# Turning q by a transposing DMA instead of TensorE, with x written in a strided order

**Chip, cores, metric.** One core of a Trainium2 chip. The metric is the device time in microseconds (us) of one execution. A profile's span is some 2 us shorter than the time of the same run.

## The reference

Attention over pooled keys and values, then a feed-forward layer with GELU. Eight batches, eight heads, 576 tokens, head dimension 64; keys and values are averaged over 8 tokens, so there are 72 of each.

```python
k_p = k.reshape(B, H, Sp, 8, D).mean(axis=3)
v_p = v.reshape(B, H, Sp, 8, D).mean(axis=3)
attn = softmax(q @ k_p^T / sqrt(D))
x = (attn @ v_p).transpose(0, 2, 1, 3).reshape(4608, 512)
out = gelu_tanh(x @ w_in) @ w_out          # w_in 512 x 2048, w_out 2048 x 512
```

## The kernel before

The second part runs in nine groups of 512 columns of x (kept transposed, as `xT`). Each group has a first layer (`w_in`, then GELU on ScalarE) and a second layer (`w_out`). Batches 1 to 7 of the attention are threaded into the groups: group g prepares batch g+1 during its first layer and computes that batch's scores, softmax and `xT` columns between the matmuls of its second layer. Batch 0 is done before group 0.

For the scores, q must lie with the head dimension on the partitions. Before, TensorE turned it, 18 transposes of 128x128 for each batch, and VectorE copied the result out of PSUM into token order:

```python
def trans_q(b, i, t0, n, bank, eng):
    if b not in qTs:
        qTs[b] = bp.tile([128, 2, 4, 32, TP], BF16, name="qT")
    tp = half_bank(bank)[:, 0:n * 128].rearrange("p (t h c) -> p h c t", h=4, c=32)
    for x in range(n):
        nc.tensor.transpose(out=half_bank(bank)[:, x * 128:(x + 1) * 128],
                            in_=qs[b][:, i, (t0 + x) * 128:(t0 + x + 1) * 128],
                            identity=identb)
    o = qTs[b][:, i, :, :, t0:t0 + n]
    ...                                    # nc.vector.tensor_copy(out=o, in_=tp)

def norm(b, c, pr, bank):                  # reciprocal of the softmax sums
    ld = ep.tile([128, CH], F32, name="ld")
    if b:
        nc.scalar.activation(out=ld[0:64], in_=PS[64:128, bank, :CH], func=ACT.Ln)
        nc.scalar.activation(out=ld[64:128], in_=PS[0:64, bank + 1, :CH], func=ACT.Ln)
    ...
    nc.scalar.activation(out=rc, in_=ld, func=ACT.Exp, scale=-1.0)

def mult(b, c, pr, bank):                  # "the multiply": writes x; CH = 288
    ...
        nc.vector.tensor_tensor(out=xT[rows, pr, col:col + CH], in0=PS[rows, bank + x, :CH],
                                in1=rc[rows], op=ALU.mult)
```

The softmax here doesn't subtract the row's maximum and nothing guards it: scores larger than these inputs give would overflow.

## Time and profile before

| | before |
|---|---|
| time, median of 3 | 320.53 us (319.16 to 321.37) |
| TensorE (PE) busy | 95% of the span |
| VectorE (DVE) busy | 55% |
| mean granted TensorE clock | 1.000 |

Page of the kernel before, costliest groups; the columns are line, engine, operation, output and inputs, shapes, count, then busy us and mean ns of one, then the engine's idle time just before them and what ended most of it:

```profile
L241 DVE TENSOR_TENSOR xT<-PS,rc 64x288 bf16<-64x288 f32 (+1 forms) x120 | 54.7, 455 | 34.5 <-ACT rc L233 24.7
```

A multiply takes 455 ns. PE's own waits in this kernel (the view of waits; us in total, times, longest):

```profile
PE PS L179 <- DMA qb<-in_q_dram: 9.6, 2, 8.9
PE PS L196 <- ACT e L202: 0.9, 3, 0.5
```

Apart from the start of the program, where the first q is awaited, and 0.7 us for the next q in group 0, PE waits for next to nothing.

### The profile page before, as it was taken

The page shows a single profiled execution, that of the slowest core. Times are in us where ns is not written, and L with a number is a line of the kernel's source. Part 1 is how long each engine was busy: PE and PEld are TensorE (multiplying, and loading weights), DVE is VectorE, ACT ScalarE, POOL GpSimd, SP SyncE. Part 2 cuts the span into 40 slices and gives each one's busy share as a digit, 9 for nine tenths or more (in the row PEclk, how much of TensorE's full clock was granted, in tenths as well). Part 3 has the DMA queues.
Part 4 walks back from the last instruction along what each step waited for, and adds up shares of the span by engine and source line. Part 5 has one row for each costly group of instructions (what it writes and reads, how often), then busy time and mean ns, then how long its engine had stood idle before and what let it go on. Part 6 is the DMA issues. An engine that isn't in the chain of part 4 may idle for free.

```text
span 318.6 us, 4265 instructions
## 1 busy us (share of the span) xinstructions
PE 301.7 (95%) x1593; PEld 156.7 (49%) x1624; DVE 176.3 (55%) x326; ACT 222.2 (70%) x414; POOL 29.5 (9%) x48
## 2 busy tenths in 40 slices
PE   0699999999999999999999999999999999999995
PEld 0456455454555455445555554555455544444442
DVE  2865836578559845974677467755776560010011
ACT  1585669967897689768985898679867987405500
POOL 8511320021001010101001100000000000000000
PEclk9999999999999999999999999999999999999999
DMA  7999999987722663174418351001200110021021
GB/s 230 262 256 261 227 259 191 248 259 175 175 74 93 165 143 107 38 221 122 125 35 222 90 147 46 0 10 59 66 2 0 66 68 0 18 83 34 0 66 66
DMA packets 17112, 37.50 MB, mean 118 GB/s; under 512 B 2020, under 2 KB 6116, under 8 KB 16196
## 3 DMA queue, kind: packets, MB, share of 16 engines
q0 software_dynamic: 10160, 24.26, 33.3%
q1 hardware_dynamic: 6708, 12.32, 12.0%
q10 hardware_dynamic: 224, 0.66, 0.5%
q8 instruction: 12, 0.20, 0.3%
q14 instruction: 8, 0.07, 0.1%
HBM read 36.70 MB, written 9.44 MB: 145 GB/s over the span
## 4 chain that ended last, share of the span: by engine, by line
PE 82%; DMA 8%; ACT 5%; POOL 3%; issue 1%; DVE 0%; ACTq 0%; POOLq 0%
PE PS L266 36%; PE PS L275 35%; DMA qb<-in_q_dram 8%; PE PS L196 4%; PE PS L215 4%; PE PS L179 2%; ACT e L202 1%; ACT ld L229 1%; ACT ld L228 1%; POOL w_in_b L101 1%; ACT gT L272 1%; PE PS L162 1%; ACT rc L233 1%; POOL kT L120 0%; POOL qb L82 0%
## 5 line engine op out<-in xcount | busy, mean ns | idle before, releaser
L266 PE MATMUL PS<-xT,w_in_b 128*128 128x512 bf16 (+2 forms) x576 | 133.8, 378 | 0.9
L275 PE MATMUL PS<-w_out_b,gT 128*128 128x512 bf16 x561 | 133.9, 379 | 0.5
L272 ACT ACTIVATE gT<-PS 128x512 bf16<-128x512 f32 x144 | 81.7, 602 | 53.3 <-PE PS L266 51.9
L266 PEld LDWEIGHTS <-w_in_b 128*128 128x128 bf16 x592 | 57.2, 99 | 60.1 <-issue 1.5
L275 PEld LDWEIGHTS <-gT 128*128 128x128 bf16 x576 | 56.0, 97 | 56.8 <-issue 0.4
L241 DVE TENSOR_TENSOR xT<-PS,rc 64x288 bf16<-64x288 f32 (+1 forms) x120 | 54.7, 455 | 34.5 <-ACT rc L233 24.7
L280 DVE COPY osb<-PS 128x512 f32<-128x512 f32 x36 | 24.9, 692 | 84.0 <-PE PS L275 84.0
L202 ACT ACTIVATE e<-PS 72x576 bf16<-72x576 f32 x64 | 40.8, 643 | 8.4 <-PE PS L196 7.5
L135 DVE TENSOR_TENSOR vt<-vt 72x1024 f32<-72x1024 f32 (+1 forms) x32 | 30.5, 952 | 0.7
L233 ACT ACTIVATE rc<-ld 128x288 f32<-128x288 f32 x64 | 28.3, 443 | 2.0
L196 PE MATMUL PS<-qT,kT 128*72 128x288 bf16 x128 | 27.6, 304 | 1.2 <-ACT e L202 0.9
L186 DVE COPY qT<-PS 128x640 bf16<-128x640 bf16 (+1 forms) x30 | 22.2, 768 | 3.3 <-PE PS L179 2.9
L228 ACT ACTIVATE ld<-PS 64x288 f32<-64x288 f32 x56 | 22.8, 407 | 1.4
L229 ACT ACTIVATE ld<-PS 64x288 f32<-64x288 f32 x56 | 22.5, 402 | 1.4
L247 ACT ACT_TABLE_LOAD x17 | 21.8, 1283 | 2.0 <-issue 1.8
L215 PE MATMUL PS<-e,vp 72*128 72x288 bf16 x112 | 23.1, 285 | 0.0
L179 PE MATMUL PS<-identb,qb 128*128 128x128 bf16 x144 | 13.9, 231 | 9.6 <-DMA qb<-in_q_dram 9.6
L196 PEld LDWEIGHTS <-kT 128*72 128x72 bf16 x128 | 15.1, 118 | 15.1 <-issue 2.1
L135 DVE TENSOR_TENSOR kt<-kt 128x1280 f32<-128x1280 f32 (+1 forms) x16 | 18.5, 1158 | 5.3 <-DMA kt<-in_k_dram 4.8
L179 PEld LDWEIGHTS <-qb 128*128 128x128 bf16 x144 | 11.2, 104 | 16.5 <-DMA qb<-in_q_dram 10.1
L168 DVE COPY kT<-PS 64x504 bf16<-64x504 bf16 x15 | 10.1, 675 | 9.4 <-PE PS L162 9.3
L215 PEld LDWEIGHTS <-vp 72*128 72x128 bf16 x112 | 11.0, 98 | 3.3
(40 smaller groups left out, 77.4 us busy)
## 6 DMA issues: line engine op xcount, KB each, us to landing
kt<-in_k_dram POOLq DMA_DIRECT2D x7, 1024.0 KB, 10.6
vt<-in_v_dram POOLq DMA_DIRECT2D x6, 1152.0 KB, 9.8
out_dram<-osb SPq DMA_DIRECT2D x24, 256.0 KB, 2.1
qb<-in_q_dram POOLq DMA_DIRECT2D x7, 576.0 KB, 10.9
w_in_b<-in_moe_w_in_dram POOLq DMA_DIRECT2D x4, 512.0 KB, 20.4
w_out_b<-in_moe_w_out_dram POOLq DMA_DIRECT2D x4, 512.0 KB, 22.2
out_dram<-osb SPq DMA_DIRECT2D x8, 192.0 KB, 2.2
vt<-in_v_dram SPq DMA_DIRECT2D x2, 576.0 KB
```

The costliest lines, as they stand in the source:

```text
L135: nc.vector.tensor_tensor(out=o, in0=a, in1=b, op=ALU.add)
L179: nc.tensor.transpose(out=half_bank(bank)[:, x * 128:(x + 1) * 128], in_=qs[b][:, i, (t0 + x) * 128:(t0 + x + 1) * 128], identity=identb)
L196: nc.tensor.matmul(out=PS[:Sp, bank + e, :CH], lhsT=kTs[b % 2][:, c, h, :], rhs=qTs[b][:, h // 4, h % 4].rearrange("p c t -> p (c t)"), st ...
L202: nc.scalar.activation(out=e, in_=PS[:Sp, bank:bank + 2, :CH], func=ACT.Exp, scale=1.0 / 64.0)
L215: nc.tensor.matmul(out=PS[:, bank + x, :CH], lhsT=flat(vps[b % 2][:, pr, x]), rhs=e[:, x, :], start=True, stop=True)
L228: nc.scalar.activation(out=ld[0:64], in_=PS[64:128, bank, :CH], func=ACT.Ln)
L229: nc.scalar.activation(out=ld[64:128], in_=PS[0:64, bank + 1, :CH], func=ACT.Ln)
L233: nc.scalar.activation(out=rc, in_=ld, func=ACT.Exp, scale=-1.0)
L241: nc.vector.tensor_tensor(out=xT[rows, pr, col:col + CH], in0=PS[rows, bank + x, :CH], in1=rc[rows], op=ALU.mult)
L266: nc.tensor.matmul(out=PS[:, h_bank(g, fo), c0:c1], lhsT=w_in_b[:, ko, fo * 128:(fo + 1) * 128], rhs=xT[:, ko, r0 + c0:r0 + c1], start=(ko ...
L272: nc.scalar.activation(out=gTs[g][:, fo, :], in_=PS[:, h_bank(g, fo), :], func=ACT.Gelu_apprx_tanh)
L275: nc.tensor.matmul(out=PS[:, o_bank(g, r), :], lhsT=gTs[g][:, fo, r * 128:(r + 1) * 128], rhs=w_out_b[:, fo, :], start=(fo == 0), stop=(fo ...
```

## The change

The intent: take 126 transposes off PE, the bound, and 28 copies off VectorE, by letting a DMA on the sync queue turn q of batches 1 to 7 while the first layer runs. The DMA gives the tokens of a chunk in another order (t, p instead of p, t). The score matmul therefore reads nine runs of 32 elements and computes its 288 columns in that order, and the multiply puts the columns back into token order as it writes `xT`. Core of the diff (the placing of some VectorE steps in the schedule is cut):

```diff
+    def trans_q_dma(b):
+        qTs[b] = bp.tile([128, 2, TP, 128], BF16, name="qT")
+        nc.sync.dma_start_transpose(out=qTs[b].rearrange("p i t c -> p (i t) c"),
+                                    in_=qs[b].rearrange("p i c -> p (i c)"))
@@ qk
-                             rhs=qTs[b][:, h // 4, h % 4].rearrange("p c t -> p (c t)"),
+                             rhs=qTs[b][:, h // 4, :, h % 4 * 32:h % 4 * 32 + 32],
@@ mult
-            nc.vector.tensor_tensor(out=xT[rows, pr, col:col + CH], in0=PS[rows, bank + x, :CH],
-                                    in1=rc[rows], op=ALU.mult)
+            nc.vector.tensor_tensor(
+                out=xT[rows, pr, col:col + CH].rearrange("p (c t) -> p t c", t=TP),
+                in0=PS[rows, bank + x, :CH].rearrange("p (t c) -> p t c", t=TP),
+                in1=rc[rows].rearrange("p (t c) -> p t c", t=TP), op=ALU.mult)
@@ group loop
-            tq = [lambda a=a, i=i: trans_q(nb, *a, 4 + i, nc.vector) for i, a in enumerate(QG)]
+            trans_q_dma(nb)
```

Successive elements of the result lie TP = 9 elements, 18 bytes, apart.

More of the change, by code (lines that the diff above doesn't have):

```diff
@@ L175, in trans_q @@
         if b not in qTs:
-            qTs[b] = bp.tile([128, 2, 4, 32, TP], BF16, name="qT")
-        tp = half_bank(bank)[:, 0:n * 128].rearrange("p (t h c) -> p h c t", h=4, c=32)
+            qTs[b] = bp.tile([128, 2, TP, 128], BF16, name="qT")
+        tp = half_bank(bank)[:, 0:n * 128].rearrange("p (t c) -> p t c", c=128)
         for x in range(n):
@@ L181, in trans_q @@
                                 identity=identb)
-        o = qTs[b][:, i, :, :, t0:t0 + n]
+        o = qTs[b][:, i, t0:t0 + n]
         if eng is nc.scalar:
@@ L186, in trans_q @@
             nc.vector.tensor_copy(out=o, in_=tp)
+    def trans_q_dma(b):
+        qTs[b] = bp.tile([128, 2, TP, 128], BF16, name="qT")
+        nc.sync.dma_start_transpose(out=qTs[b].rearrange("p i t c -> p (i t) c"),
+                                    in_=qs[b].rearrange("p i c -> p (i c)"))
     QG = [(0, 0, 5), (0, 5, 4), (1, 0, 5), (1, 5, 4)]
@@ L195, in qk @@
             h = 2 * pr + e
-            nc.tensor.matmul(out=PS[:Sp, bank + e, :CH], lhsT=kTs[b % 2][:, c, h, :],
-                             rhs=qTs[b][:, h // 4, h % 4].rearrange("p c t -> p (c t)"),
+            nc.tensor.matmul(out=PS[:Sp, bank + e, :CH].rearrange("j (t p) -> j t p", p=32),
+                             lhsT=kTs[b % 2][:, c, h, :],
+                             rhs=qTs[b][:, h // 4, :, h % 4 * 32:h % 4 * 32 + 32],
                              start=True, stop=True)
@@ L335 @@
             v0, v1 = v_steps(nb, 0), v_steps(nb, 1)
-            tq = [lambda a=a, i=i: trans_q(nb, *a, 4 + i, nc.vector) for i, a in enumerate(QG)]
+            trans_q_dma(nb)
             tk = [lambda: trans_k(nb, 4)]
             if g:
-                plan = {2: kk[:1], 3: kk[1:], 4: tq[:1], 5: tq[1:2], 6: tq[2:3], 7: tq[3:],
-                        9: tk, 10: v0[:1], 11: v0[1:], 12: v1[:1], 13: v1[1:]}
+                plan = {2: kk[:1], 3: kk[1:], 7: v0[:1], 8: v0[1:], 9: tk, 11: v1[:1], 12: v1[1:]}
             else:
-                plan = {1: v0, 2: v1, 7: kk, 8: tq[:1], 9: tq[1:2], 10: tq[2:3], 11: tq[3:], 13: tk}
+                plan = {1: v0, 2: v1, 7: kk, 12: tk}
             for fo, what in plan.items():
```

## The prediction

> **What bounds the kernel now.** I read the page first for the busy shares and the chain that ended last, then the PE timeline of one steady group, then the same stretch of group 0, where the loads are still coming in, and last the landing times of transfers.
>
> ```profile
> PE 301.7 (95%) x1593; PEld 156.7 (49%) x1624; DVE 176.3 (55%) x326; ACT 222.2 (70%) x414; POOL 29.5 (9%) x48
> ...
> PE 82%; DMA 8%; ACT 5%; POOL 3%; issue 1%; DVE 0%; ACTq 0%; POOLq 0%
> ```
>
> PE is the bound and DVE is not: PE has no idle slice after the start and makes up 82% of the chain. So DVE time that is removed is worth nothing by itself, and PE time that is removed is worth its full length, as long as nothing new makes PE wait. In nanoseconds per row PE durations overlap (a 512-column matmul shows 379 ns, but eight follow each other in 1.73 us, 216 ns apart), so I take the cost of the transposes from start times. In a steady group (the timeline of PE, first columns start and length):
>
> ```profile
> 132.28 0.44 PE L179 MATMUL PS<-identb,qb 128*128 128x128 bf16 x5
> 132.56 1.03 PE L266 MATMUL PS<-xT,w_in_b 128*128 128x512 bf16 x4
> 133.42 0.39 PE L179 MATMUL PS<-identb,qb 128*128 128x128 bf16 x4
> 133.64 1.03 PE L266 MATMUL PS<-xT,w_in_b 128*128 128x512 bf16 x4
> 134.50 0.44 PE L179 MATMUL PS<-identb,qb 128*128 128x128 bf16 x5
> ```
>
> Five transposes push the next matmul by 132.56 - 132.28 = 0.28 us, four by 133.64 - 133.42 = 0.22 us. The reader is to see that 18 transposes cost 2 x 0.28 + 2 x 0.22 = 1.0 us, not 18 x 231 ns = 4.2 us. Group 0 has one more thing, a wait for the load of q of batch 1:
>
> ```profile
> 36.10 0.45 PE L179 MATMUL PS<-identb,qb 128*128 128x128 bf16 x5 [0.73 <-DMA qb<-in_q_dram]
> ...
> 44.73 0.41 PE L196 MATMUL PS<-qT,kT 128*72 128x288 bf16 x2
> ```
>
> That load lands at 36.1 us and its first score matmul runs at 44.73 us. How long a transfer from the sync queue takes depends on when it is sent. These are the stores of 256 KB (last column: us from issue to landing), first in the stretch 36 to 60 us, then from 125 us to the end:
>
> ```profile
> out_dram<-osb SPq DMA_DIRECT2D x2, 256.0 KB, 12.2
> ...
> out_dram<-osb SPq DMA_DIRECT2D x16, 256.0 KB, 2.0
> ```
>
> The same store takes six times as long while the software queue is full of loads. The view by stretches shows the DMA engines oversubscribed (share 1.20) from 36 to 43.4 us, 1.01 from 43.4 to 61.6, 0.89 from 61.6 to 77, and about 0.45 in the later groups.
>
> **What the Trainium skill says.** "VectorE: DVE Perf Modes", section "The three transpose paths", lists 390 ns for TensorE and 1309 ns for the DMA crossbar per 128x128 block; the trace has 219 to 231 ns for one TensorE transpose and 56 ns between starts, so here the matmul way is far cheaper than listed. No transposing DMA is in the trace. "DMA: Bandwidth & Descriptors", section "Latency and other measured facts", gives 261 GB/s for one transposing kernel; its section "DMA Transpose (X-bar)" puts one crossbar tile at 16 partitions by 128 elements. Its section "Queues, rings and completion order" says that each DMA engine takes turns between queues packet by packet; the 12.2 against 2.0 us above agree with a sync transfer that gets a turn only between packets of a long software backlog. "SBUF — State Buffer", section on the DMA port swizzle, warns of a penalty for accesses that step to a new 16-byte line each time. The trace speaks mildly against it for VectorE: the qT copies read PSUM 256 bytes apart and write runs of five, and still take 820 ns for 640 elements and 716 ns for 512, about 0.8 ns per further element.
>
> **The change, part by part.**
>
> Removed from PE: 18 transposes in each of seven groups, 7 x 1.0 = 7.0 us, all on the path. Also the 0.7 us wait of group 0 at 36.1 us. Together 7.7 us, which is 2.4% of 320.5. This is the ceiling.
>
> Removed from DVE: 28 copies of 768 ns, 21.5 us, all off the path, worth nothing. The POOL wait for these transposes before the next q load turns into a wait for the DMA transpose; those loads come a whole group early, so it is worth nothing either.
>
> The score matmul reads 9 runs of 32 elements in place of 288 in a row; a run is 64 bytes, so whole lines are used. I expect no change (0.12 us between starts). The multiply writes x with a step of 18 bytes. I expect 455 ns as now, by the qT copies. If it slowed by 0.3 us, only the four multiplies right after a group's end matter: they end 2.8 us after the next first-layer matmuls begin (127.70 to 130.50), and the columns of the second half are needed in groups 1 to 3 only. That would be 3 x 1.2 = 3.6 us at most.
>
> Added: seven transposing DMAs of 576 KB. In groups 1 to 6 one is issued behind the last store of the group before, about 0.9 us after the group's start, and needed by the first score matmul, at 144.35 us for a group begun at 127.70: 16.65 us, less the 1.0 us saved, less 0.9, so a window of 14.8 us. The engines are almost idle early in that window (share 0.16 from 128 to 134 us). At 261 GB/s the estimate is 2.3 us plus about 2 us, the landing of a small transfer. Even three times this is hidden.
>
> In group 0 the window is short. q lands at 36.1; the scores would be due at 44.73 - 0.73 - 1.0 = 43.0 us, a window of 6.9 us. There are 144 crossbar tiles, nine for each of 16 engines, an estimate from the skill's tile size. The 256 KB store has eight rows of 2 KB per engine and took 12.2 us in this crowd, 1.5 us a turn. Nine turns give 13.7 us, by bytes (36 KB against 16 KB an engine) it would be 27 us, on quiet engines about 5. I choose 13: landing at 49, a PE stall of 6 us. Nothing later gives it back, as PE is the bound in every later group.
>
> Sum: 320.5 - 7.0 - 0.7 + 6 = 318.8; the stall drains the backlog somewhat, so that group 1 stays hidden; I say 318.5.
>
> **The rivals.**
>
> First: everything is hidden. For it: most score windows are 15 us, and SBUF to SBUF needs no HBM. Against it: the 12.2 us stores in the crowded stretch. It would make 320.5 - 7.7 = 312.8.
>
> Second: the transposing DMA is slow in itself. If 18 blocks of 1309 ns ran one after another they would take 23.6 us, 9 us over the window in each of six groups and 17 or more in group 0: 320.5 - 7 + 54 + 17 = 385. For it: small pieces, 32 bytes per partition and tile on the writing side, and nobody in this trace shows its rate. Against it: 32 KB in 1309 ns looks like one engine's pace, and there are 16. A milder case, 17 us, costs about 2 us a group and 10 us at the start: 320.5 - 7.7 + 12 + 10 = 335.
>
> Third: DVE's strided write or PE's broken reads are slower. At most 3.6 us for the first, as above; it would eat half the gain and leave about 316 to 322 depending on group 0.
>
> **Range and chances.** Faster by over 2% means below 314.1: at least 6.4 of the 7.7 us must remain, so group 0 may stall 1.3 us at most, that is its transpose must land within about 8 us in a stretch where a smaller store took 12. I give 0.22. Slower by over 2% means above 326.9, which needs a group 0 transpose over 21 us or a steady one over 16 us: 0.25. Between them 0.53. The range is 312.5 (everything hidden) to 334 (the milder slow case).
>
> **What would show it.** Right: PE without the q transposes but for batch 0, first matmuls of groups 2 to 6 without gaps and each such group 1.0 us shorter (33.1 to 32.1 us), the transposes landing inside 15 us there, over 10 us in group 0, with one PE wait of 3 to 9 us on qT near 43 us. The multiplies stay near 455 ns and the score matmuls near 0.12 us apart. Wrong: a wait on qT in every group (the second rival), no wait in group 0 (the first), multiplies of 600 ns or more (the third), or stores held up behind a transpose in the sync queue so long that a copy out of PSUM waits for its buffer.

## The result

| | before | after |
|---|---|---|
| time, median | 320.95 us (4 runs) | 432.51 us (4 runs) |
| PE busy | 95% | 73% |
| VectorE busy | 55% | 63% |
| the multiply | 455 ns | 1434 ns |
| mean granted TensorE clock | 1.000 | 0.925 |

The ratio is 1.3485 (95% interval 1.342 to 1.3551). The change costs 112 us; 318.5 was predicted and 334 was the top of the range.

Page of the kernel after: busy times, then the chain that ended last by engine, then the group of the multiplies:

```profile
PE 315.9 (73%) x1470; PEld 150.5 (35%) x1498; DVE 270.3 (63%) x298; ACT 222.4 (52%) x414; POOL 29.6 (7%) x48
...
PE 41%; DVE 35%; DMA 10%; issue 7%; ACT 7%; ACTq 0%; DVEq 0%
...
L247 DVE TENSOR_TENSOR xT<-PS,rc 64x288 bf16<-64x288 f32 (+1 forms) x120 | 170.0, 1434 | 42.8 <-PE PS L221 34.5
```

VectorE, absent from the chain before, now makes up 35% of it, and one line does most of that: the multiply (30% of the chain by the page), three times as long. PE's waits after:

```profile
PE PS L221 <- DVE xT L247: 42.3, 42, 1.2
PE PS L201 <- DMA qT<-qb: 26.4, 1, 26.4
PE PS L274 <- DVE xT L247: 25.8, 13, 3.1
...
PE PS L226 <- DVE xT L247: 1.4, 2, 0.8
```

There are two separate losses. The first is 42.3 + 25.8 + 1.4 = 69.5 us of waiting for multiplies: L221, the matmul with v, waits for the PSUM bank that a multiply still reads, and L274, the first layer of the next group, waits for columns of x. The second is one single wait of 26.4 us for the transposed q, in group 0. What a steady second layer looks like, busy us of each engine in one such stretch, before and after (then the granted clock, the DMA share and GB/s):

```profile
143.06:160.83 17.77, 17.66 (x96) 9.60 (x97) 9.07 (x19) 15.89 (x32) 0.86 (x1) 1.00 0.42 111
```

```profile
207.85:233.29 25.44, 18.98 (x95) 9.51 (x96) 19.18 (x15) 16.50 (x34) 0.39 (x1) 1.00 0.31 78
```

The same 96 or so matmuls take 25.44 instead of 17.77 us. The third figure with a count is VectorE: 19.18 us of work with fewer instructions, where there were 9.07. VectorE has become the bound of this stage: from its first multiply on, at 213.57 us, its timeline has no gap until 232.5 us. The first part of it:

```profile
213.57 5.80 DVE L247 TENSOR_TENSOR xT<-PS,rc 64x288 bf16<-64x288 f32 x4 [0.64 <-ACT rc L239]
219.41 0.69 DVE L288 COPY osb<-PS 128x512 f32<-128x512 f32 x1
220.13 5.80 DVE L247 TENSOR_TENSOR xT<-PS,rc 64x288 bf16<-64x288 f32 x4
```

And the transposing DMA itself, us from issue to landing, in the stretch 30 to 40 us (group 0), then the median over all seven:

```profile
qT<-qb SPq DMA_TRANSPOSE x1, 34.5
```

```profile
qT<-qb SPq DMA_TRANSPOSE x7, 5.1
```

On quiet engines it is nearly as fast as predicted (4.3 us). In group 0 it takes 34.5 us where 13 was guessed and the window was about 7. PE, which had nothing else to do, found its clock at half when it came back: in the profile's stretches the granted clock is 0.50 from 49.3 to 69 us and 0.86 from 69 to 80.

Of the 112 us, 69.5 + 26.4 are waits that the view names and 7.7 were saved as planned. Some 24 us more are left by subtraction. Most of that is the lower clock, which came with both faults: in each later group, too, it is at 0.50 for 3.4 or 6.8 us, about when PE's wait for columns of x ends (239.4 to 242.8 us, for one). Over the ten stretches at 0.50 in the change PE is busy for 35.4 us by the view by stretches. Half of that, 17.7 us, is an estimate of what the clock cost; some 6 us stay open. The kernel before had a mean clock of 1.000.

### The profile page after: what moved, and what is told of

Its sections match the earlier page's. It is cut to its first block, busy times and chain, and to the rows that moved or that the text cites. A ratio compares the mean times of both kernels' runs of the same rounds, so it can differ in the third digit from the quotient of the medians.

```text
span 430.2 us, 3997 instructions
## 1 busy us (share of the span) xinstructions
PE 315.9 (73%) x1470; PEld 150.5 (35%) x1498; DVE 270.3 (63%) x298; ACT 222.4 (52%) x414; POOL 29.6 (7%) x48
## 4 chain that ended last, share of the span: by engine, by line
PE 41%; DVE 35%; DMA 10%; issue 7%; ACT 7%; ACTq 0%; DVEq 0%
DVE xT L247 30%; PE PS L274 24%; PE PS L283 13%; DMA qT<-qb 8%; DVE osb L288 3%; ACT e L208 2%; ACT rc L239 2%; ACT ld L234 2%; DMA kt<-in_k_dram 2%; PE PS L201 1%; ACT ld L235 1%; PE PS L221 1%; DVE vt L135 1%; PE PS L162 1%; DVE kt L135 1%
## 5 line engine op out<-in xcount | busy, mean ns | idle before, releaser
L247 DVE TENSOR_TENSOR xT<-PS,rc 64x288 bf16<-64x288 f32 (+1 forms) x120 | 170.0, 1434 | 42.8 <-PE PS L221 34.5
L274 PE MATMUL PS<-xT,w_in_b 128*128 128x512 bf16 (+2 forms) x579 | 141.6, 400 | 26.6 <-DVE xT L247 25.8
L283 PE MATMUL PS<-w_out_b,gT 128*128 128x512 bf16 x561 | 136.1, 384 | 0.8 <-issue 0.2
L274 PEld LDWEIGHTS <-w_in_b 128*128 128x128 bf16 x592 | 60.6, 104 | 102.6 <-issue 31.8
L221 PE MATMUL PS<-e,vp 72*128 72x288 bf16 x112 | 29.6, 286 | 44.2 <-DVE xT L247 42.3
L201 PE MATMUL PS<-qT,kT 128*72 128x288 bf16 x128 | 27.1, 296 | 27.9 <-DMA qT<-qb 26.4
L168 DVE COPY kT<-PS 64x504 bf16<-64x504 bf16 x15 | 10.1, 675 | 17.9 <-PE PS L162 17.8
L70 POOL DMA_DIRECT2D kt<-in_k_dram x7 | 4.0, 574 | 143.6 <-DVE kp L135 141.5
L221 PEld LDWEIGHTS <-vp 72*128 72x128 bf16 x112 | 10.5, 99 | 9.1 <-issue 5.1
L179 PE MATMUL PS<-identb,qb 128*128 128x128 bf16 x18 | 2.3, 311 | 8.8 <-DMA qb<-in_q_dram 8.8
L82 POOL DMA_DIRECT2D qb<-in_q_dram x9 | 6.4, 710 | 29.7 <-DMA qT<-qb 28.5
```

The costliest lines, as they stand in the source:

```text
L201: nc.tensor.matmul(out=PS[:Sp, bank + e, :CH].rearrange("j (t p) -> j t p", p=32), lhsT=kTs[b % 2][:, c, h, :], rhs=qTs[b][:, h // 4, :, h ...
L221: nc.tensor.matmul(out=PS[:, bank + x, :CH], lhsT=flat(vps[b % 2][:, pr, x]), rhs=e[:, x, :], start=True, stop=True)
L247: nc.vector.tensor_tensor(out=xT[rows, pr, col:col + CH].rearrange("p (c t) -> p t c", t=TP), in0=PS[rows, bank + x, :CH].rearrange("p (t ...
L274: nc.tensor.matmul(out=PS[:, h_bank(g, fo), c0:c1], lhsT=w_in_b[:, ko, fo * 128:(fo + 1) * 128], rhs=xT[:, ko, r0 + c0:r0 + c1], start=(ko ...
L283: nc.tensor.matmul(out=PS[:, o_bank(g, r), :], lhsT=gTs[g][:, fo, r * 128:(r + 1) * 128], rhs=w_out_b[:, fo, :], start=(fo == 0), stop=(fo ...
```

## Experiments

The theories at this point. **W**: a scattered two-byte write is slow by itself. Rivals: **R**, the three-dimensional operands or their reads cost it; **C**, collisions with TensorE's reads or with DMA do. **Q**: the transpose of group 0 is slow because its pieces wait their turn among the loads of the software queue (those that GpSimd issues); rivals: **S**, a start-up cost, and **X**, the crossbar (what does the transposing in the DMA) suffers beside other traffic. All runs gave correct results. e1, e7, e8, e9 and e12 are one run each and are read for single operations, not for their total time.

### e1: the multiply by itself

Appended behind the last store of the kernel before, where nothing else runs, on scratch tiles:

```diff
+    for _ in range(4): nc.vector.tensor_tensor(out=bx[:, 0:CH], in0=bp0, in1=ba, op=ALU.mult)
+    # and 18 more: result in the change's order; reads in steps, write dense (both inputs, PSUM
+    # alone, SBUF alone); bf16 at steps 2, 3, 4, 8, 9, 16; f32 at steps 2, 4, 9; pairs and fours
+    # 16 bytes apart; a VectorE cast and two ScalarE casts
```

> The kernel before, with 19 small VectorE and ScalarE operations on scratch appended after its last store, four of each, on quiet engines: the multiply of 64x288 with its result written dense, in the order of the change (18 bytes from element to element), at other steps and in float32, with strided reads and a dense write, and copies. Theory W (the scattered two-byte write is slow by itself): dense 455 ns, the change's write 1430 ns with nothing else running, strided reads with a dense write near 455 ns. Rival R (the three-dimensional operands or the reads cost it): strided reads with a dense write are slow too. Rival C (collisions with TensorE reads or DMA): the change's write is near 455 ns here. Among the steps: if a new 16-byte line per element is what costs, steps of 2 and 4 elements (4 and 8 bytes) are fast or in between and 8 and more are slow; if any separate two-byte write costs, 2 is as slow as 9.

Durations in ns (min/median/max), one line for each variant. In order: dense; the change's order; both inputs in steps of 128 bytes with a dense write; only the PSUM input so; only the SBUF input so; bf16 at steps of 2, 4 and 8 elements; f32 at a step of 4 elements (16 bytes); pairs of bf16 16 bytes apart; ScalarE dense and in the change's order:

```profile
L408 DVE TENSOR_TENSOR by<-PS,ba x4: 449/449/450, 316.9 to 318.3; 64x288 bf16<-64x288 f32 x4
L409 DVE TENSOR_TENSOR by<-PS,ba x4: 1411/1412/1412, 318.8 to 323.1; 64x288 bf16<-64x288 f32 x4
L410 DVE TENSOR_TENSOR by<-PS,ba x4: 623/624/625, 324.6 to 326.6; 64x288 bf16<-64x288 f32 x4
L411 DVE TENSOR_TENSOR by<-PS,ba x4: 449/449/450, 327.2 to 328.7; 64x288 bf16<-64x288 f32 x4
L412 DVE TENSOR_TENSOR by<-PS,ba x4: 623/625/626, 329.2 to 331.1; 64x288 bf16<-64x288 f32 x4
L413 DVE TENSOR_TENSOR by<-PS,ba x4: 470/470/471, 331.8 to 333.3; 64x288 bf16<-64x288 f32 x4
L415 DVE TENSOR_TENSOR by<-PS,ba x4: 786/787/789, 336.5 to 338.9; 64x288 bf16<-64x288 f32 x4
L416 DVE TENSOR_TENSOR by<-PS,ba x4: 1422/1423/1424, 339.8 to 344.1; 64x288 bf16<-64x288 f32 x4
L420 DVE TENSOR_TENSOR by<-PS,ba x4: 652/657/658, 358.8 to 360.9; 64x288 f32<-64x288 f32 x4
L422 DVE TENSOR_TENSOR by<-PS,ba x4: 449/449/451, 364.4 to 365.8; 64x288 bf16<-64x288 f32 x4
L425 ACT CAST by<-PS x4: 392/392/392, 374.0 to 375.3; 64x288 bf16<-64x288 f32 x4
L426 ACT CAST by<-PS x4: 1408/1408/1409, 375.7 to 380.0; 64x288 bf16<-64x288 f32 x4
```

W holds: 1412 ns with every other engine idle, so C falls; the reads explain at most 175 ns, so R falls for the bulk. Three things were new. Steps through PSUM are free, steps through float32 in SBUF are not (449 against 625). ScalarE suffers as VectorE does (392 to 1408). And pairs of bf16 in separate 16-byte lines cost nothing, while singles cost everything: it is not the new line alone. That became e12. (Seven of the 19 variants are not shown here.)

### e12: half words

```diff
+    # pairs 16 bytes apart, on a word, then shifted by one element; threes 16 bytes apart;
+    # 144 and 72 single elements 18 bytes apart; 288 singles in the upper half of a word
```

> Six more multiplies on scratch behind the kernel before, all writing bf16 with f32 inputs. Theory H (a four-byte word of which only one half is written costs about 4.4 ns for each 16-byte line touched): pairs on a word, 16 bytes apart, 449 ns; the same pairs shifted by one element, so that each fills two half words, about 790; threes 16 bytes apart about 575; 144 single elements 18 bytes apart about 790 and 72 about 470; 288 single elements 16 bytes apart, in the upper half of the word, 1420. Theory L (the new line costs, not the half word): shifted pairs and threes 449.

In order: pairs on a word, shifted pairs, threes, 144 singles:

```profile
L407 DVE TENSOR_TENSOR by<-PS,ba x4: 450/450/451, 315.8 to 317.3; 64x288 bf16<-64x288 f32 x4
L408 DVE TENSOR_TENSOR by<-PS,ba x4: 787/787/789, 317.8 to 320.2; 64x288 bf16<-64x288 f32 x4
L409 DVE TENSOR_TENSOR by<-PS,ba x4: 576/577/579, 321.0 to 322.9; 64x288 bf16<-64x288 f32 x4
L410 DVE TENSOR_TENSOR by<-PS,ba x4: 776/778/779, 323.5 to 325.9; 64x144 bf16<-64x144 f32 x4
```

A pair that fills a four-byte word: 450 ns. The same pair shifted so that it fills two halves: 787. Theory H holds in every variant (72 singles gave 466, the upper half 1422). VectorE's bf16 results of the two runs fit one rule, worked out from them: time = 150 ns + the larger of 1.04 ns per element and 4.4 ns per 16-byte line in which some four-byte word is only half written. (Singles 4, 6, 8 and 16 bytes apart touch 72, 108, 144 and 288 lines and took 470, 630, 787 and 1423 ns.) For the change that is 150 + 288 x 4.4 = 1417. The largest miss is singles 32 bytes apart, 1354 ns. It is no rule for float32: singles 16 and 36 bytes apart took 657 and 660 ns, where it gives 450. Why the hardware does so, no run shows; the word and line sizes are read off the pattern of times.

### e2: the changed kernel with a dense write

```diff
-                out=xT[...].rearrange("p (c t) -> p t c", t=TP),
-                in0=PS[...].rearrange("p (t c) -> p t c", t=TP),
-                in1=rc[rows].rearrange("p (t c) -> p t c", t=TP), op=ALU.mult)
+                out=xT[...].rearrange("p (c t) -> p c t", t=TP),
+                in0=PS[...].rearrange("p (t c) -> p c t", t=TP),
+                in1=rc[rows].rearrange("p (t c) -> p c t", t=TP), op=ALU.mult)
```

The same values land in the same places; only the order in which the elements are visited changes.

> The changed kernel, but the multiply walks its operands in the order of x: dense write, strided reads of PSUM and of the reciprocals. Same values. Theory W: the multiply returns to about 455 ns, some 90 us go, and what is left over the kernel before is the stall of group 0 (26 us, and about 1 us of half clock after it) less 7 us of transposes: about 340 us. Rival R: it stays over 400 us, as reads cost the same.

The multiplies of this run:

```profile
L247 DVE TENSOR_TENSOR xT<-PS,rc 64x288 bf16<-64x288 f32 (+1 forms) x120 | 77.3, 644 | 57.9 <-PE PS L221 38.2 <-ACT rc L239 16.2 <-PE PS L226 1.2
```

347.21 us, ratio 1.0833 (1.0789 to 1.0876). A single reordering gives back 85 us. The multiply was 644 ns instead of the expected 455, because the reciprocals in SBUF are now read with a step (e1: 625), and PE waited 30.1 us for q in group 0, where the transpose took 37.0 us to land. So the estimate of 340 was 7 short, for those two reasons as far as the trace shows.

### e3: the strided write alone

The change with every q turned by TensorE (in the DMA's order) and the schedule of before; x written strided as in the change.

> The x half of the change alone: x written strided in the change's order, q of all batches turned by TensorE (written in the DMA's order, so that the score matmul reads the broken runs), the schedule of before. Theory W: multiply 1430 ns, about 320.5 + 90 = 410 us. If the DMA half caused most of the loss instead, this is near 320 us.

Two of the four runs (412.18 and 413.47 us) are slow. The two fast ones took 404.35 and 409.44 us, where the kernel before had 320.25 in the same rounds, so 84 to 89 us slower with no DMA transpose at all. PE waits 43.5 us for multiplies at L221 and 24.5 at L274, nearly the waits of the change. The write costs 84 to 89 us, and the change with a dense write still 27 (e2); together 111 to 116, so the two account for the whole 112.

### e4: batch 1 by TensorE, the rest by DMA

Dense write as in e2; batch 1 turned by TensorE.

> Dense write as in the second run, and batch 1 turned by TensorE as before, so that only batches 2 to 7 use the transposing DMA. If the two faults are the strided write and the crowded transpose of group 0, and nothing else, all that stays is the saving of 6 x 1.0 us: about 314.5 us, with no wait on qT. If it is over 318, a third cost is in the change (score matmuls reading broken runs, loads delayed).

330.51 us, ratio 1.0306 (1.0256 to 1.0356), not 314.5. The fault had moved: with group 0 no longer stalled, batch 2's transpose now fell into the crowd. It was issued at 62.3 us and PE got going again at 86.95, after a wait of 9.56 us:

```profile
86.95 0.66 PE L201 MATMUL PS<-qT,kT 128*72 128x288 bf16 x2 [9.56 <-DMA qT<-qb]
```

In the change itself batch 2 had been fine: the stall in group 0 had let the loads drain, and the software queue moved no packet from 90 to 100 us, when that transpose began.

### e7, e8, e9: what makes the transpose slow in a crowd

The kernel before, in which PE does not need the added transfer (only a later load of q can wait for it, 23.4 us in e8), with one transfer from the q tile to a spare tile at the start of group 0 and another in group 5. Only its kind differs:

```diff
+    # e7   nc.sync.dma_start_transpose(out=spare, in_=q tile)
+    # e8   nc.sync.dma_start(out=spare[:, :, 0:128], in_=q tile as 18 blocks of 128)  # 256-byte pieces
+    # e9   nc.sync.dma_start(out=spare, in_=q tile)                                   # 4608-byte rows
```

> The kernel before, with one transposing DMA added in group 0 and one in group 5 on the sync queue, from the q tile into a spare tile that nobody reads. Theory Q: over 25 us to land in group 0, about 5 us in group 5; the total about as before.

> The same two places, but a plain copy of the same bytes in 2304 pieces of 256 bytes in place of the transpose. Theory Q says that the number of pieces, each waiting a turn, makes the time: over 25 us in group 0, about 5 us in group 5, like the transpose. Rival X (the crossbar itself is slow beside other traffic): much shorter in group 0, under 15 us.

> The same two places again, a plain copy of the same 576 KB in whole rows of 4608 bytes, so some eight pieces for each engine. Theory Q: few turns, so about the 12 us that the 256 KB stores took in group 0, or less, and about 3 us in group 5. If the bytes and not the pieces set the time, it takes over 25 us in group 0.

us from issue to landing, group 0 first and then group 5, for e7, e8 and e9 in turn:

```profile
spare<-qb SPq DMA_TRANSPOSE x1, 37.0
spare<-qb SPq DMA_TRANSPOSE x1, 4.8
```

```profile
spare<-qb SPq DMA_DIRECT2D x1, 576.0 KB, 28.9
spare<-qb SPq DMA_DIRECT2D x1, 576.0 KB, 4.6
```

```profile
spare<-qb SPq DMA_DIRECT2D x1, 576.0 KB, 6.7
spare<-qb SPq DMA_DIRECT2D x1, 576.0 KB, 3.0
```

The same bytes in 256-byte pieces without any transposing take 28.9 us in the crowd; in long rows 6.7. So Q holds for the bulk of group 0: the number of pieces sets most of the time, not the bytes, and no transposing is needed for 28.9 of the 37.0 us. The transpose is still 8 us slower than the plain pieces; the sync engine is held 14.2 us by its issue there, against 0.7 for the plain copy. The packets of the change between 34.5 and 69 us say the same: queue 1 moved

```profile
q1 hardware_dynamic: 2336, 0.59, 30.0%
```

that is 2336 packets for 0.59 MB, 252 bytes each, 146 for each of 16 engines; 34.5 us over 146 is 0.24 us a turn. Quiet, 5.1 over 146 is 0.035.

X does not fall altogether. The last figure of the line above is the time that the packets themselves took: 30.0% of 34.5 us on 16 engines is 71 ns a packet, against 26 ns in the quiet stretch from 142.7 to 148 us. The plain pieces of e8 took 24 ns in the crowd (37 to 48 us) and quiet (196.9 to 202 us), and only waited. In e4, while batch 2 was being turned, the two queues had from 73.1 to 86 us

```profile
q1 hardware_dynamic: 1126, 0.28, 77.7%
q0 software_dynamic: 152, 1.05, 24.5%
```

so a packet of the transpose took 142 ns while the loads used a quarter of the engines' time. A turn among many loads does not explain that stall; what lengthens these packets stays open.

### e6: hold the loads back instead

All seven batches by DMA; a one-column copy on GpSimd reads the transposed q before the loads for batch 2 and 3 are issued. The operands are ordered as in e5.

> Same order of operands, all seven batches by DMA, but the loads for batches 2 and 3 are held back until the transpose of batch 1 and of batch 2 has landed. Theory Q (the transpose waits its turn behind the software queue's loads): both land in a few us once only the rest of the output weights is in front of them, say 8 to 15 us for batch 1 and about 5 for batch 2; total 320.5 - 7.7 + 2 to 6 = 315 to 319 us. Rival S (the first transpose is slow for another reason, such as a start-up cost): batch 1 still takes over 25 us and the total is near 335 us.

320.42 us, ratio 1.0000 (0.9962 to 1.0038). Group 0's transpose:

```profile
qT<-qb SPq DMA_TRANSPOSE x1, 13.6
```

It landed in 13.6 us instead of 34.5 and its wait fell to 6.0 us: rival S falls, and an intervention shows that the loads cause most of it (by turns or by longer packets, this run does not tell apart). But the output weights are still being loaded there, so a stall and some half-clock remain (0.54 from 48.2 to 52 us), and they eat the saving.

### e11: the order without any DMA

The columns in the DMA's order with every q turned by TensorE, the operands ordered as in e5.

> The columns in the DMA's order with dense writes and strided PSUM reads, but every q turned by TensorE, with the schedule of before. If the broken runs of the score matmul and the strided PSUM reads cost nothing, this is 320.3 us, the same as before, and all that the fifth and tenth runs gain comes from the transposes taken off PE. If it is 323 or more, the order itself has a price.

320.30 us, ratio 0.9977 (0.9931 to 1.0024): the broken reads of the score matmul and the strided PSUM reads cost nothing.

### e5: both faults avoided

Batches 1 and 2 by TensorE, 3 to 7 by DMA. The reordering is moved to where it is free, the reads of PSUM:

```diff
-            nc.scalar.activation(out=ld[0:64], in_=PS[64:128, bank, :CH], func=ACT.Ln)
+            nc.scalar.activation(out=asx(ld[0:64]), in_=asc(PS[64:128, bank, :CH]), func=ACT.Ln)
@@ mult                          # asx: "p (c t) -> p c t" (dense), asc: "p (t c) -> p c t" (in steps)
+                out=asx(xT[rows, pr, col:col + CH]), in0=asc(PS[rows, bank + x, :CH]),
+                in1=asx(rc[rows]), op=ALU.mult)
```

> Both faults avoided: the reordering moved to the reads of PSUM (the logarithm reads PSUM in the order of x and writes dense, so that the multiply reads only PSUM with a step and reads its other operand and writes x dense), batches 1 and 2, whose transposes fall into the crowded stretch, turned by TensorE, batches 3 to 7 by the transposing DMA. If strided PSUM reads are free as the first run showed, the multiply takes 455 ns and the logarithm stays at 405 ns. Then 5 x 1.0 us are saved: about 315.5 us, no wait on qT. If the DMA or the broken score reads have a further cost, it stays at 318 or more.

316.15 us, ratio 0.9867 (0.981 to 0.9924). The multiply is back at 455 ns, ScalarE's logarithms stay at 407 and 402 ns, and PE has no wait on the transposed q.

### e10: one batch by TensorE, six by DMA

Batch 1 by TensorE; the loads of batch 3 held back until batch 2's transpose has landed; operands as in e5.

> As the fifth run, but batch 2 is turned by DMA too, and the loads of batch 3 are held until that transpose has landed; only batch 1 is turned by TensorE. Theory Q: the transpose of batch 2 lands in about 5 to 10 us, no PE wait on qT, and 6 x 1.0 us are saved: about 314.5 us. If it still takes over 16 us, PE waits and the total is no better than the fifth run's 316.

314.54 us (313.67 to 316.49), ratio 0.9811 (0.9764 to 0.9859). The transposes of this run, us to landing (min/median/max):

```profile
DMA to landing us min/median/max: 4.8/5.1/5.5
```

All six land in about 5 us, batch 2's too. The time is 6.0 us under the 320.53 that the prediction started from, and 6.6 under the median of the same rounds: six transposed batches at 1.0 us each. This version beats both kernels. Its gain over the kernel before is clear of zero, but the interval straddles 2%.

## Why the prediction was wrong, point by point

- **Removed from PE, 1.0 us per batch: right.** e5 saves 4.2 us for five batches by its medians, e10 6.6 for six, e11 nothing for none clear of noise (0.8). One steady group of e10 lasts 32.1 us (125.52 to 157.64), of the kernel before 33.1, as predicted.
- **The strided write, "I expect 455 ns as now, by the qT copies": wrong, and the step that failed most.** It measured 1434 ns, worth 84 to 89 us of time (e3). The copies I argued from wrote runs of four or five bf16. By the rule of e12, if it holds for copies, each of the 128 runs of five leaves one half-written word, 150 + 128 x 4.4 = 713 ns, under the 816 ns that the rule gives for 640 elements anyway: such a copy cannot show the cost. Nor were these copies free, as I took it from their 0.8 ns per further element: with dense reads and writes the same copies take 490 and 420 ns in e11, against 820 and 716. There was no dense copy in the trace to compare with, and which step slowed them, in the read or the write, no run separates. Writing one element to a line, the case at hand, was in nothing that I had measured, and I gave it a bound of 0.3 us taken from nowhere.
- **"Only the four multiplies right after a group's end matter": wrong as a consequence.** It held while VectorE had slack. At 1434 ns, 16 multiplies and four copies of 692 ns are 25.7 us in a second layer that took 17.8, so VectorE became the bound there, and 43.7 of the 69.5 us of waits (L221 and L226) lie inside the layer.
- **The transpose on quiet engines, about 4.3 us: right** (5.1), and hidden in every steady group, as said. The second rival, 18 blocks one after another in 23.6 us, was wrong.
- **The transpose in group 0, "nine turns" of 1.5 us: right in mechanism for the most part, wrong in size.** It takes its turns among the loads (e6 to e9), but I counted a whole tile as one turn: it is 146 pieces of some 256 bytes per engine at 0.24 us, 34.5 us, not nine and 13.7. That a packet of the transpose itself takes longer in a crowd (71 against 26 ns) was not in the prediction. The stall was 26.4 us, not 6. The estimate of 27 us by bytes came closer by accident: e9 moves the same bytes in 6.7.
- **Broken reads of the score matmul, no change: right** (e11).
- **The chances:** 0.25 for slower, and nothing beyond 334 but for the serial rival. The two faults together were in no scenario; the third rival was capped at 3.6 us on the strength of the same failed step. The sign that the prediction named for that rival, multiplies of 600 ns or more, is the one that came.

## What to carry to other kernels

Before an output pattern with a step goes onto a loaded engine, measure that very pattern: a neighbour that writes short runs proves nothing about single bf16 elements, and where data must be reordered, try it in the read of PSUM with a dense write (449 ns here, as with no reordering). A transfer of many small pieces was cheap on quiet DMA engines and very slow beside a backlog of loads (4.6 against 28.9 us in e8), so look where in the program it falls, not at its median; moving the first one out of the crowd can push the next one in. A saving on the bound is worth its full length only as long as no other engine crosses its own limit in the same stage.

## What the Trainium skill lacked or had wrong

- "VectorE: DVE Perf Modes", section "Mode 1× (REGULAR) — the baseline", gives this mode one result per cycle and says that odd strides and PSUM operands all work in it. For bf16 results written singly 16 or 18 bytes apart the runs show 1423 and 1412 ns for 288 elements, against 449 dense; the half-word rule (4.4 ns per 16-byte line with a half-written word, pairs on a word free at 450 ns, shifted pairs 787) is on no page that I read.
- "SBUF — State Buffer", section on the DMA port swizzle, warns of a penalty for each new 16-byte line, in the right direction; it does not say that it is small for whole words (657 ns for float32 at 16 bytes, 625 for a float32 read in steps) and large for half words (1423 at 16 bytes, and 787 at 8 bytes, two to a line). It also says that PSUM patterns that are not contiguous slow matmuls, and nothing there of VectorE, whose reads of PSUM in steps of 128 bytes cost nothing (449 ns); no run here has such a matmul.
- "DMA: Bandwidth & Descriptors", section "DMA Transpose (X-bar)", speaks of 256-byte source rows but does not say that the transposing DMA goes out in packets of that size (2336 packets for 0.59 MB) or what that means beside a loaded queue: 34.5 us against about 5 on quiet engines, with packets that themselves took 71 ns against 26. The page's 261 GB/s (section "Latency and other measured facts") would be, as an estimate, 2.3 us for 576 KB plus about 2 us for the landing of a small transfer, which agrees with the 4.8 to 5.5 us of e10.
